# Gated attention in fp32 split products: attention's order from another table, outer sums around the gate's step, first attention loads a step later

## The chip, the cores and the metric

One core of one Trainium2 chip runs the kernel. TensorE (PE) multiplies matrices into PSUM, VectorE (DVE), ScalarE (ACT) and GpSimd (POOL) do elementwise work, SyncE (SP) issues most DMA transfers. The metric is the device time of one execution in microseconds; the text gives the median of the runs.

## The reference

x is 2048 x 640, there are 32 heads of 128, and attention reads the last 512 of 2048 cached positions (W = max(256, 2048 // 4)). Everything is float32.

```python
xn = layernorm(x)                                   # no weights, eps 1e-5
q  = (xn @ wq) as 32 heads of 128
p  = softmax(q @ k[:, -512:].T * 128**-0.5)         # no mask
s  = (p @ v[:, -512:]) as 2048 x 4096 @ wo
h  = relu(xn @ w1 + b1) ** 2                        # 640 -> 1728
g  = silu(h @ w2 + b2)                              # 1728 -> 640
out = x + s * g
```

## The kernel before, in words

Each float32 operand is split into a rounded part (hi, tile index 0) and the remainder (lo, index 1), and each product is three matmuls, hi·hi + hi·lo + lo·hi (`triple`). The hi parts are made by ScalarE copies, the lo parts by a subtraction on VectorE or POOL. All matmuls are 128x128 by 128x512, and 512 rows of x are one tile, so there are four.

The program has three stages. **First**, layer norm and the feed-forward part: the up products of tile 0, then those of tiles 1 and 2 in a seven-product scheme, and the down products of tiles 1 and 2. The down products are the loop over m from 0 to 27 (14 chunks of w2 for tile 1, then 14 for tile 2; `c_down`), called steps below. A step is 15 matmuls into five PSUM banks py. Its operands ch (a block of h) and cw (a block of w2) are loaded three steps ahead on SyncE (`c_load`) and split two steps ahead on ScalarE and VectorE (`c_prep`). Behind step 13 stands `gate`: for each of five banks a sigmoid on ScalarE and a multiply on VectorE into sg. Step 14 writes the same banks, so it waits for sg.

Beside these steps the loop makes the outer tiles: sums of x's tiles 0 and 3 that attention's scheme for q needs (`outer_sum`, six subtractions or additions per part q on VectorE; `outer_hi`, a copy on ScalarE; `outer_lo`, a subtraction on VectorE and two stores to memory). There are two parts, each with its own load (`outer_load`, four DMAs of 0.26 MB). The dictionary OUTER says which of them runs at which step. After the last, their memory becomes the pool "ep", into which attention's first operands are loaded (x as ax, wq as qr, k as kr; `load_raw`, `load_xT`), before attention's first product q_mm(0), which stands ahead of step 27.

**Second**, attention: 128 units (two halves of the rows x 16 groups of two heads x two row tiles x two heads), each 12 matmuls of scores s into two banks, softmax (maxima by VectorE, gathered by ScalarE, exp on ScalarE, the split of p into pt by ScalarE and POOL) and 12 matmuls o. Every second unit adds five products r with wo, added to acc. q comes from the same seven-product scheme, group by group: products into banks pq..a and pq..b, between them a copy qp of b, a copy of a into b (`q_seed`), and sums `q_add`, `q_sum` (qu) on VectorE. In the first half POOL and ScalarE also prepare the sums of wq (gr, zs) for the second half.

**Third**, the feed-forward part of tile 3, and the output.

The order in attention is set by a plan: each operation gets a time, `at(when, f, *a)`, in periods of 12.4 per unit, plus offsets from the table K; operations are recorded sorted by that time, and each engine keeps its recorded order (class Ordered). The times are no measured times: they only set the order. For q_seed:

```python
on(key("Q4", 8.3), q_seed, n)
```

where `key` adds the offsets K["Q4" + ...] for the third of the run, the place in the group and the unit. Every operation is issued through Ordered, so line 322 of the profile is nearly all of them; the groups are told apart by their tiles.

Of the kernel before, what the change touches and what calls it, by code (L numbers as in the profile page):

```python
# [11 lines left out]
ALU = mybir.AluOpType  # L12
# [12 lines left out]
K = {  # L25
# [68 lines left out]
    "ZK3": 0.45, "ZKa": -0.8, "ZKb": 1.81, "ZKc": 7.72, "ZKd": 3.31, "ZKe": 4.57, "ZL0": -0.89,  # L94
    "ZL1": -1.83, "ZL2": -1.23, "ZL3": 0.77, "ZLa": 0.33, "ZLb": 2.02, "ZLc": 6.28, "ZLd": 0.51,
# [173 lines left out]
def kernel(  # L269
# [20 lines left out]
    DC = D // P  # L290
# [876 lines left out]
    for q in range(NQ2):  # L1167
# [4 lines left out]
        if q == 0:  # L1172
            steps += [(len, ())] * int(K.get("OG", 0))
# [1153 lines left out]
```

## Time and profile before

| | us |
|---|---|
| median of 3 runs | 1945.45 |
| lowest, highest | 1944.21, 1947.82 |
| profiled execution, its own time | 1943.89 |
| its span | 1942.1 |
| TensorE busy | 1921.4 |
| VectorE busy | 1673.9 |
| POOL busy | 1490.1 |
| ScalarE busy | 1423.8 |

Busy times are of the whole span. The profile's rows name an operation as out<-in with the buffers' numbers left out, so pq, o, r and s are the products described above and py those of the down steps. "x12" is a count. In the timeline a row gives the start, the duration, the engine, and in brackets how long the engine sat idle before and for whom.

### The profile page before, as it was taken

The numbers are of one execution on the slowest core, as the hardware profiler recorded it, in microseconds if no ns is written. First come the engines' busy times: TensorE is split into PE (matmuls) and PEld (weight loads), VectorE is DVE, ScalarE is ACT, GpSimd is POOL, SyncE is SP. The second block draws the span as 40 slices with busy tenths as digits, with TensorE's granted clock in tenths as the row PEclk, the third lists the DMA queues.
The fourth block names the chain that finished last, engine by engine and source line by source line (L and its number), as shares of the span: only waits on it lengthen the run. The fifth ranks groups of instructions, "written<-read, shape, count | busy, mean of one in ns | idle before, by whom it ended". The sixth has DMA issues, their size and how long they took to land. (4 is left out here: it accounts for less than half of the span.)

```text
span 1942.1 us, 30037 instructions
## 1 busy us (share of the span) xinstructions
PE 1921.4 (99%) x8405; PEld 1563.8 (81%) x8405; DVE 1673.9 (86%) x2451; ACT 1423.8 (73%) x3096; POOL 1490.1 (77%) x963
## 2 busy tenths in 40 slices
PE   9999999999999999999999999999999999999998
PEld 7888778778888888888887788888888888888887
DVE  6864756899999999999999889999999999999865
ACT  5665536888888888888887788777777777777743
POOL 1022116999999999999998888999998888888952
PEclk9999999999999999999999999999999999999999
DMA  6866885654444444444457632333332222222455
GB/s 204 275 216 215 302 320 185 201 161 146 148 147 147 147 147 147 147 147 147 147 159 236 197 112 75 106 106 106 106 116 85 85 85 85 85 85 87 140 167 199
DMA packets 195409, 296.97 MB, mean 153 GB/s; under 512 B 19044, under 2 KB 100726, under 8 KB 194230
## 3 DMA queue, kind: packets, MB, share of 16 engines
q1 hardware_dynamic: 190102, 275.77, 44.2%
q0 software_dynamic: 5008, 19.14, 2.5%
q8 instruction: 77, 1.26, 0.3%
q14 instruction: 78, 0.64, 0.1%
q10 hardware_dynamic: 144, 0.16, 0.0%
HBM read 219.49 MB, written 75.51 MB: 152 GB/s over the span
## 5 line engine op out<-in xcount | busy, mean ns | idle before, releaser
L322 POOL TENSOR_TENSOR pt<-e,pt 128x1024 fp32r<-128x1024 f32 x256 | 616.8, 2409 | 87.5 <-ACT pt L322 85.2
L322 PE MATMUL r<-ots,wo 128*128 128x512 f32 x1920 | 489.5, 391 | 1.2 <-ACT acc L322 0.8
L322 PEld LDWEIGHTS r<-ots,wo 128*128 128x128 f32 x1920 | 357.9, 188 | 82.6 <-DVE acc L322 5.4
L322 PE MATMUL o<-pt,wv 128*128 128x512 f32 x1536 | 380.2, 391 | 0.5 <-POOL pt L322 0.4
L322 PE MATMUL s<-q,wk 128*128 128x512 f32 x1536 | 374.4, 391 | 0.2 <-DVE q L322 0.2
L322 PEld LDWEIGHTS o<-pt,wv 128*128 128x128 f32 x1536 | 285.5, 188 | 67.4 <-POOL pt L322 8.7
L322 DVE TRANSPOSE_TENSOR_REDUCE rdm<-s 128x32 f32<-128x1024 f32 x256 | 311.6, 1236 | 32.5 <-PE s L322 26.1
L322 PEld LDWEIGHTS s<-q,wk 128*128 128x128 f32 x1536 | 285.9, 188 | 65.8 <-DVE q L322 5.0
L322 POOL TENSOR_TENSOR e<-e,e 128x1024 f32<-128x1024 f32 x128 | 308.1, 2407 | 8.5
L322 DVE TENSOR_TENSOR e<-s,bm 128x1024 f32<-128x1024 f32 x256 | 302.5, 1183 | 1.9 <-POOL pt L322 0.6
L322 ACT ACTIVATE e<-e 128x1024 f32<-128x1024 f32 x256 | 270.2, 1056 | 45.0 <-DVE e L322 43.9
L322 ACT ACTIVATE pt<-e 128x1024 fp32r<-128x1024 f32 x256 | 270.7, 1057 | 9.7 <-PE o L322 0.2
L322 DVE TENSOR_TENSOR acc<-r,acc 128x512 f32<-128x512 f32 x300 | 198.8, 663 | 11.7 <-PE r L322 11.3
L322 ACT ACTIVATE rdm<-rdm 32x64 f32<-32x64 f32 x384 | 97.8, 255 | 123.1 <-DVE rdm L322 118.1
L322 DVE TRANSPOSE_TENSOR_REDUCE rds<-e 128x32 f32<-128x1024 f32 (+1 forms) x128 | 124.3, 971 | 28.3 <-POOL e L322 27.7
L322 ACT ACTIVATE rowm<-rowm 32x16 f32<-32x16 f32 x384 | 82.2, 214 | 63.9 <-DVE rowm L322 59.7
L322 ACT ACTIVATE rds<-rds 32x32 f32<-32x32 f32 (+1 forms) x384 | 89.3, 232 | 42.4 <-DVE rds L322 37.7
L322 ACT ACTIVATE rows<-rows 32x16 f32<-32x16 f32 x384 | 82.2, 214 | 34.0 <-DVE rows L322 26.5
L322 PE MATMUL py<-ch,cw 128*128 128x512 f32 x410 | 97.3, 399 | 6.6 <-ACT cw L322 4.5
L322 PEld LDWEIGHTS py<-ch,cw 128*128 128x128 f32 x410 | 78.7, 193 | 24.8 <-ACT cw L322 4.9
L322 POOL TENSOR_TENSOR wo<-or,wo 128x640 fp32r<-128x640 f32 x62 | 97.7, 1575 | 0.9 <-ACT wo L322 0.9
L322 DVE STREAM_TRANSPOSE bm<-rowm 128x512 f32<-128x512 f32 x128 | 87.3, 682 | 12.0 <-ACT rowm L322 10.6
(642 smaller groups left out, 3175.9 us busy)
## 6 DMA issues: line engine op xcount, KB each, us to landing
qp<-wq_d SPq DMA_DIRECT2D x60, 640.0 KB
qp<-wq_d SPq DMA_DIRECT2D x60, 512.0 KB
or<-in_wo_dram SPq DMA_DIRECT2D x62, 320.0 KB
kr<-in_kT_dram SPq DMA_DIRECT2D x62, 256.0 KB
vr<-in_v_dram SPq DMA_DIRECT2D x62, 256.0 KB
wq_d<-ots SPq DMA_DIRECT2D x112, 128.0 KB
gr<-in_wq_dram SPq DMA_DIRECT2D x32, 320.0 KB
wq_d<-gr SPq DMA_DIRECT2D x80, 128.0 KB
```

What stands on the lines that cost most here:

```text
L322: ins = method(*args, **kwargs)
```

## The change

Three things.

The table K has other numbers: offsets for the same operations of attention and of the last stage. Their set of operations is the same, their order is not.

OUTER is written out by step. Part 0 runs at steps 10, 11, 12, 14 and 15, part 1 at 17 to 21; before, they were laid out three at a time from step 10 on, so part 0 also had three operations at step 13, ahead of the gate. The second load comes at step 12 instead of 15.

Attention's first loads come one step later, behind the loads for steps 26 and 27, and each tile of x comes in two parts (columns 0 to 2, then 3 and 4) at steps 23 to 26. Before, x's first tile was loaded whole at step 22 and its second at 24.

```diff
 K = {
-    "Q412": 5.0, "Q42": 2.37, "Q422": 0.73, "Q4@10": 1.41, "Q4@122": 3.21, "Q4@58": 1.52,
+    8.97, "Q42": 0.4, "Q422": 2.63, "Q4@10": 1.79, "Q4@122": 1.93, "Q4@58": 0.11, "Q4@6": -2.14,
...
-    steps = []
-    for q in range(NQ2):
-        steps += [(outer_sum, q, k) for k in range(3)]
-        steps += [(outer_hi, q, 0), (outer_sum, q, 3), (outer_sum, q, 4), (outer_hi, q, 1)]
-        steps += [(outer_lo, q, 0), (outer_sum, q, 5), (outer_hi, q, 3), (outer_lo, q, 1), (outer_hi, q, 2)]
-        steps += [(outer_lo, q, 3), (outer_lo, q, 2)]
-        if q == 0:
-            steps += [(len, ())] * int(K.get("OG", 0))
-    first_m, per = int(K.get("OM", 11)), K.get("OP", 3.0)
-    for n, w in enumerate(steps):
-        OUTER.setdefault(int(first_m + n / per), []).append(w)
+    OUT0, OUT1 = 10, 17
+    for q, first in enumerate((OUT0, OUT1)):
+        for n, *w in (
+            *((0, outer_sum, q, k) for k in range(3)),
+            *((1, outer_hi, q, 0), (1, outer_sum, q, 3), (1, outer_sum, q, 4)),
+            *((2, outer_hi, q, 1), (2, outer_lo, q, 0), (2, outer_sum, q, 5)),
+            *((4 - q, outer_hi, q, 3), (4 - q, outer_lo, q, 1), (4 - q, outer_hi, q, 2)),
+            *((5 - q, outer_lo, q, 3), (5 - q, outer_lo, q, 2)),
+        ):
+            OUTER.setdefault(first + n, []).append(tuple(w))
...
-        if m == first_m + int((len(steps) / per + K.get("OG", 0) / per) / 2) - 1 + int(K.get("OX", 0)):
+        if m == OUT0 + 2:
             outer_load(1)
-        if m == OPEN + int(K.get("OO", 0)):
-            for f, *a in [w for n, l in sorted(OUTER.items()) if n >= m for w in l]:
-                f(*a)
-            OUTER.clear()
+        if m == OPEN + 1:
+            assert not OUTER
             octx.close()
             pools["ep"] = ctx.enter_context(tc.tile_pool(name="early", bufs=1, side="right"))
+        n = m - OPEN - 1
+        if n == 1:
             load_raw("q", 0, 0)
             load_raw("k", 0, 0)
             open_xT(0, 0)
+        for t, c in {0: ((0, slice(0, 3)),), 1: ((0, slice(3, DC)),), 2: ((1, slice(0, 3)),), 3: ((1, slice(3, DC)),)}.get(n - 1, ()):
+            if (t, c.start) == (1, 0):
+                open_xT(0, 1)
             for i in range(2):
-                load_xT(0, 0, i, slice(0, DC))
-        if m == OPEN + 2 + int(K.get("OO", 0)):
+                load_xT(0, t, i, c)
+        if n == 2:
             for kind in "qk":
                 prep(kind, 0, 0, dve)
                 load_raw(kind, 0, 1)
-            open_xT(0, 1)
-            for i in range(2):
-                load_xT(0, 1, i, slice(0, DC))
-        if m == OPEN + 4 + int(K.get("OO", 0)):
+        if n == 4:
```

OPEN is 21; the table before had OM 10, OG 6 and OO 1. The engines and queues that the table could choose for these operations are written in, the same ones.

Three places show what moves. The first is VectorE ahead of the gate, before (to is an outer tile, ch15 and cw15 are the operands of step 15, sg the gate's result):

```order
L322 TENSOR_TENSOR to021_2406<-xc3_2_2268,xc3_0_2148 128x512
L322 TENSOR_TENSOR ch15_1_2507<-ch15_2469,ch15_0_2506 128x512
L322 TENSOR_TENSOR cw15_1_2511<-cw15_2467,cw15_0_2510 128x640
L322 TENSOR_TENSOR to011_2404<-to011_2404,to010_2403 128x512
L322 SCALAR_TENSOR_TENSOR sg_2535<-py1_0_2087,b_sb_65,sg_2535 128x512
L322 SCALAR_TENSOR_TENSOR sg_2539<-py1_1_2088,b_sb_65,sg_2539 128x512
L322 SCALAR_TENSOR_TENSOR sg_2543<-py1_2_2089,b_sb_65,sg_2543 128x512
```

and with the change:

```order
L322 TENSOR_TENSOR to021_2406<-xc3_2_2268,xc3_0_2148 128x512
L322 TENSOR_TENSOR ch15_1_2512<-ch15_2469,ch15_0_2511 128x512
L322 TENSOR_TENSOR cw15_1_2516<-cw15_2467,cw15_0_2515 128x640
L322 SCALAR_TENSOR_TENSOR sg_2535<-py1_0_2087,b_sb_65,sg_2535 128x512
L322 SCALAR_TENSOR_TENSOR sg_2539<-py1_1_2088,b_sb_65,sg_2539 128x512
L322 SCALAR_TENSOR_TENSOR sg_2543<-py1_2_2089,b_sb_65,sg_2543 128x512
L322 SCALAR_TENSOR_TENSOR sg_2547<-py1_3_2090,b_sb_65,sg_2547 128x512
L322 SCALAR_TENSOR_TENSOR sg_2551<-py1_4_2091,b_sb_65,sg_2551 128x512
L322 TENSOR_TENSOR ch16_1_2561<-ch16_2509,ch16_0_2560 128x512
L322 TENSOR_TENSOR cw16_1_2565<-cw16_2507,cw16_0_2564 128x640
L322 TENSOR_TENSOR to011_2404<-to011_2404,to010_2403 128x512
```

The subtraction for to011 stood ahead of sg and now stands behind the operands of step 16.

The second is SyncE around attention's first loads, before:

```order
L322 DMA cw25_2820<-in_w2_dram 128x640
L322 DMA ch25_2822<-h_m2_11_204 128x512
L322 DMA qr0_0_2836<-in_wq_dram 128x640
L322 DMA kr0_0_2838<-in_kT_dram 128x512
L322 DMA ax0_0_0_2840<-xT_d0_0_66 128x2560
L322 DMA ax0_0_1_2841<-xT_d0_1_67 128x2560
L322 DMA cw26_2859<-in_w2_dram 128x640
L322 DMA ch26_2861<-h_m2_12_205 128x512
L322 DMA cw27_2863<-in_w2_dram 128x640
L322 DMA ch27_2865<-h_m2_13_206 128x512
L322 DMA qr0_1_2901<-in_wq_dram 128x640
L322 DMA kr0_1_2907<-in_kT_dram 128x512
```

and with the change:

```order
L322 DMA cw25_2820<-in_w2_dram 128x640
L322 DMA ch25_2822<-h_m2_11_204 128x512
L322 DMA cw26_2851<-in_w2_dram 128x640
L322 DMA ch26_2853<-h_m2_12_205 128x512
L322 DMA cw27_2855<-in_w2_dram 128x640
L322 DMA ch27_2857<-h_m2_13_206 128x512
L322 DMA qr0_0_2867<-in_wq_dram 128x640
L322 DMA kr0_0_2869<-in_kT_dram 128x512
L322 DMA ax0_0_0_2871<-xT_d0_0_66 128x1536
L322 DMA ax0_0_1_2872<-xT_d0_1_67 128x1536
L322 DMA ax0_0_0_2871<-xT_d0_0_66 128x1024
L322 DMA ax0_0_1_2872<-xT_d0_1_67 128x1024
```

The loads for steps 26 and 27 stood behind x's first tile (ax0_0) and now stand ahead of qr, kr and x, and x comes in smaller pieces.

The third is ScalarE in attention, unit 26, before (pq7b<-pq7a is q_seed for group 7, e the exponentials, pt their hi part):

```order
L322 ACTIVATE e26_0_6702<-e26_0_6702 128x1024
L322 ACTIVATE pt26_0_0_6720<-e26_0_6702 128x1024
L322 ACTIVATE e26_1_6718<-e26_1_6718 128x1024
L322 ACTIVATE qp57_6726<-pq7b_6651 128x512
L322 ACTIVATE pt26_1_0_6729<-e26_1_6718 128x1024
L322 ACTIVATE pq7b_6732<-pq7a_6668 128x512
L322 ACTIVATE ots0_3064<-zs8_2_6700 128x2x128
```

and with the change:

```order
L322 ACTIVATE e26_0_6712<-e26_0_6712 128x1024
L322 ACTIVATE pt26_0_0_6722<-e26_0_6712 128x1024
L322 ACTIVATE qp57_6728<-pq7b_6657 128x512
L322 ACTIVATE e26_1_6730<-e26_1_6730 128x1024
L322 ACTIVATE pq7b_6742<-pq7a_6666 128x512
L322 ACTIVATE pt26_1_0_6750<-e26_1_6730 128x1024
L322 ACTIVATE ots0_3068<-zs8_2_6704 128x2x128
```

The copy qp57 moved ahead of e26_1, and pq7b ahead of pt26_1_0. Two moves go the other way: on TensorE the three matmuls pq9a<-ax0_0 of group 9 (and their like in 12 groups of the first half) moved from behind the six of r33_0 to directly behind s36_2, and on VectorE qu324 (and its like in 13 groups of the second half) moved from ahead of the lo part of ots2 to behind it.

More of the change, by code (lines that the diff above doesn't have):

```diff
@@ L25 @@
 K = {
[68 rows of a table removed]
-    "ZK3": 0.45, "ZKa": -0.8, "ZKb": 1.81, "ZKc": 7.72, "ZKd": 3.31, "ZKe": 4.57, "ZL0": -0.89,
-    "ZL1": -1.83, "ZL2": -1.23, "ZL3": 0.77, "ZLa": 0.33, "ZLb": 2.02, "ZLc": 6.28, "ZLd": 0.51,
[169 rows of a table removed]
[67 rows of a table added]
+    1.27, "ZHc": 5.54, "ZHd": -16.51, "ZHe": 4.38, "ZK1": 1.35, "ZK2": -2.2, "ZK3": 0.71, "ZKa":
+    -0.77, "ZKb": 2.09, "ZKc": 8.07, "ZKd": 3.54, "ZKe": 5.95, "ZL0": -1.19, "ZL1": 0.06, "ZL2":
+    -1.49, "ZL3": 1.69, "ZLa": -0.05, "ZLb": 0.49, "ZLc": 4.46, "ZLd": 2.86, "ZLe": 4.2, "ZR0":
[169 rows of a table added]
 }
@@ L1126, in outer_load @@
             for i in range(2):
-                (pool, sp)[int(K.get("OLX", 0))].dma_start(XO[q][:, j, i, :], xT_d[0][i][:, NQ2 * j + q, :])
+                sp.dma_start(XO[q][:, j, i, :], xT_d[0][i][:, NQ2 * j + q, :])
     def outer_tiles(q):
@@ L1150, in outer_sum @@
         )[k]
-        ENG["o"].tensor_tensor(out, one, two, op=op)
+        dve.tensor_tensor(out, one, two, op=op)
     def outer_hi(q, j):
@@ L1158, in outer_lo @@
         hi, lo = TO[q][j]
-        ENG["l"].tensor_tensor(lo, raw(lo), raw(hi), op=ALU.subtract)
+        dve.tensor_tensor(lo, raw(lo), raw(hi), op=ALU.subtract)
         for i in range(2):
-            (pool, sp)[int(K.get("OLS", 0))].dma_start(TS_d[0][j][:, q, i, :], raw(TO[q][j][i]))
+            pool.dma_start(TS_d[0][j][:, q, i, :], raw(TO[q][j][i]))
     XO, TO = {}, {}
-    ENG = {"o": (dve, pool)[int(K.get("OE", 0))], "l": (dve, pool)[int(K.get("OL", 0))]}
     OUTER = {}
-    steps = []
-    for q in range(NQ2):
-        steps += [(outer_sum, q, k) for k in range(3)]
-        steps += [(outer_hi, q, 0), (outer_sum, q, 3), (outer_sum, q, 4), (outer_hi, q, 1)]
-        steps += [(outer_lo, q, 0), (outer_sum, q, 5), (outer_hi, q, 3), (outer_lo, q, 1), (outer_hi, q, 2)]
-        steps += [(outer_lo, q, 3), (outer_lo, q, 2)]
-        if q == 0:
-            steps += [(len, ())] * int(K.get("OG", 0))
-    first_m, per = int(K.get("OM", 11)), K.get("OP", 3.0)
-    for n, w in enumerate(steps):
-        OUTER.setdefault(int(first_m + n / per), []).append(w)
+    OUT0, OUT1 = 10, 17
[8 more added lines that the diff above has]
+            OUTER.setdefault(first + n, []).append(tuple(w))
     XT, ACC, KT, VV, WQ, WO, Q, E, SC, MB, RD, PT, PO, OT, RB, QPS, FX, CL, PRS, RAW = (
@@ L1881 @@
             pools["to"] = octx.enter_context(tc.tile_pool(name="outer", bufs=1, side="right"))
-        if m == first_m - 2 + int(K.get("OX0", 0)):
+        if m == OUT0 - 2:
             outer_load(0)
-        if m == first_m + int((len(steps) / per + K.get("OG", 0) / per) / 2) - 1 + int(K.get("OX", 0)):
+        if m == OUT0 + 2:
             outer_load(1)
-        if m == OPEN + int(K.get("OO", 0)):
-            for f, *a in [w for n, l in sorted(OUTER.items()) if n >= m for w in l]:
-                f(*a)
-            OUTER.clear()
+        if m == OPEN + 1:
+            assert not OUTER
             octx.close()
             pools["ep"] = ctx.enter_context(tc.tile_pool(name="early", bufs=1, side="right"))
+        n = m - OPEN - 1
+        if n == 1:
             load_raw("q", 0, 0)
```

471 rows, old and new, of the table K are left out of this document.

## The prediction

> **What bounds the kernel now.** I read the page first, then the waits of TensorE, then its windows, and only where these showed lost time the timeline.
>
> ```profile
> span 1942.1 us, 30037 instructions
> ...
> PE 1921.4 (99%) x8405; PEld 1563.8 (81%) x8405; DVE 1673.9 (86%) x2451; ACT 1423.8 (73%) x3096; POOL 1490.1 (77%) x963
> ```
>
> TensorE is the bound: 99% busy with 8405 matmuls, whose number the change leaves alone. So the change can win only time in which TensorE waits or runs at half clock, and can lose only by new waits. Where it waits (us in total, times, longest):
>
> ```profile
> PE py L322 <- ACT cw L322: 4.5, 1, 4.5
> PE py L322 <- DVE sg L322: 1.9, 1, 1.9
> ...
> PE pq16a L322 <- DVE qu L322: 1.0, 1, 1.0
> PE r L322 <- ACT acc L322: 0.8, 2, 0.6
> ...
> PE pq2a L322 <- ACT pq2b L322: 0.4, 1, 0.4
> ```
>
> This list understates. A matmul is drawn 0.39 us long, but back to back they start 0.227 apart (below: 42 in 9.68 us, so 9.29 / 41), so each wait costs 0.16 more than it shows, and one below 0.16 shows nothing. I therefore count matmuls by window, attention alone (330 to 1905 us; a row gives the stretch, its length, busy us and count of TensorE, its weight loads, VectorE, ScalarE and POOL, then granted clock, DMA share and GB/s):
>
> ```profile
> 330.00:395.00 65.00, 63.71 (x276) 51.13 (x275) 53.81 (x74) 55.83 (x130) 60.61 (x41) 1.00 0.62 194
> 395.00:990.00 595.00, 593.92 (x2583) 478.06 (x2582) 561.81 (x786) 479.08 (x1111) 557.17 (x383) 1.00 0.47 146
> 990.00:1160.00 170.00, 167.93 (x730) 135.10 (x729) 153.87 (x218) 133.47 (x305) 149.35 (x96) 1.00 0.58 183
> 1160.00:1535.00 375.00, 375.00 (x1646) 307.62 (x1645) 342.28 (x498) 290.59 (x637) 340.34 (x183) 1.00 0.31 99
> 1535.00:1635.00 100.00, 100.00 (x442) 82.54 (x441) 92.56 (x135) 76.50 (x169) 88.37 (x47) 1.00 0.27 91
> 1635.00:1905.00 270.00, 269.76 (x1187) 221.77 (x1186) 232.29 (x330) 186.50 (x401) 218.18 (x120) 1.00 0.36 117
> ```
>
> A window also counts matmuls that hang over its edge, 1.7 of them (0.39 / 0.227). The fifth window is the pace: 100 / (442 - 1.7) = 0.2271 us. By that pace the others should take 62.3, 586.2, 165.4, 373.4 and 269.2 us; they take 2.7, 8.8, 4.6, 1.6 and 0.8 more: **18.5 us** that attention loses in small pieces.
>
> **The change part by part.** *First loads a step on, x in four parts.* The longest wait stands ahead of step 26 of the down loop:
>
> ```profile
> 261.77 19.20 PE L322 MATMUL py<-ch,cw 128*128 128x512 f32 x84
> ...
> 271.00 0.33 SPq L322 DMA_DIRECT2D qr<-in_wq_dram  x1
> ...
> 271.86 0.90 SPq L322 DMA_DIRECT2D ax<-xT_d  x2
> ...
> 273.28 0.43 SPq L322 DMA_DIRECT2D ch<-h_m  x1
> ...
> 284.13 0.63 ACT L322 ACTIVATE ch<-ch 128x512 fp32r<-128x512 f32 x1 [12.81 <-DMA ch<-h_m]
> ...
> 285.44 5.19 PE L322 MATMUL py<-ch,cw 128*128 128x512 f32 x15 [4.47 <-ACT cw L322]
> ...
> 293.88 3.56 PE L322 MATMUL py<-ch,cw 128*128 128x512 f32 x15
> ```
>
> The load of ch for step 26 is issued behind two loads of x of 1.31 MB each (128x2560 in four bytes), and ScalarE waits 12.81 us for it. In the change SyncE issues the loads for steps 26 and 27 ahead of qr, kr and all of x. The wait goes: 4.47 + 0.16, and with it the slow run behind it, 5.19 - 3.56 = 1.63. **6.2 us**; between 3.6 (x still slows what is left, and the half clock stays) and 6.3.
>
> What is late next is x itself, for attention's first product, which stands behind step 26.
>
> ```profile
> 237.40:240.84 3.44, 1.56 (x7) 1.16 (x7) 3.44 (x6) 3.44 (x7) 2.76 (x6) 1.00 0.97 257
> 240.84:244.25 3.41, 3.41 (x9) 2.68 (x9) 3.41 (x6) 1.07 (x2) 1.18 (x3) 0.50 1.03 396
> ...
> 1080.50:1083.90 3.40, 2.37 (x11) 1.67 (x10) 3.40 (x6) 1.67 (x6) 3.40 (x2) 1.00 0.92 313
> 1083.90:1087.30 3.40, 3.40 (x16) 2.79 (x16) 3.17 (x7) 1.86 (x8) 3.32 (x5) 1.00 0.24 78
> ...
> 273.00:285.00 12.00, 7.97 (x36) 6.26 (x34) 0.21 (x1) 0.87 (x2) 0.00 (x0) 1.00 0.96 368
> ```
>
> The last of these rows: DMA moves 368 GB/s when it is full. qr, kr (0.33 and 0.26 MB) and the first tile of x, 2.62 MB, are 3.2 MB, so 8.7 us. SyncE is held until 271.00, when the outer tiles' memory is free; that stays about so (one pair more of their stores moves to the last step, about 1 us). So x is in at about 281. Step 26 without its wait ends at 280.97 + 15 x 0.227 = 284.4, or 282 with the gate's gain below. A margin of 1 to 3 us, and each us that x is late costs one: between 0 and 2, I take 0. The second tile of x follows by 290, before the third unit needs it.
>
> *The gate's step without outer sums.* Step 14 waits for the first sg:
>
> ```profile
> 227.82 9.68 PE L322 MATMUL py<-ch,cw 128*128 128x512 f32 x42
> ...
> 237.24 0.82 DVE L322 TENSOR_TENSOR cw<-cw,cw 128x640 fp32r<-128x640 f32 x1
> ...
> 237.98 0.69 DVE L322 TENSOR_TENSOR to<-to,to 128x512 fp32r<-128x512 f32 x1
> ...
> 238.58 3.38 DVE L322 SCALAR_TENSOR_TENSOR sg<-py,b_sb,sg 128x512 f32<-128x512 f32 x5
> ...
> 239.38 6.92 PE L322 MATMUL py<-ch,cw 128*128 128x512 f32 x22 [1.88 <-DVE sg L322]
> ```
>
> VectorE runs without a gap here, and only the "to" operation leaves its row ahead of sg: sg starts at 237.98, 0.6 sooner. ScalarE loses two operations there too and has its half of sg ready. So the wait shrinks from 1.88 to about 1.3. The 22 matmuls behind it took 6.92 where pace gives 21 x 0.227 + 0.39 = 5.16: 1.76 lost to the half clock in the second window row above. Does the half clock stay? After an idle of 1.88 in a 3.4 us window it came, after 1.03 (the row at 1080.50) it did not. 1.3 is nearer to 1.03, so I count it as gone: 0.6 + 1.8 = **2.4 us**, between 0.6 and 3.8.
>
> The Trainium skill (TensorE: Matmul & The Clock Gate, "What's actually happening") has the clock drop after at least one idle window of about 3.4 us. By that rule neither 1.88 nor 1.3 would halve it; the trace disagrees with the first (0.50 after 1.88). By the rule the term would be 0.6 with nothing to win back, by the row 2.4; the row decides.
>
> The second outer load also moves, from step 15 to 12: 1.05 MB ahead of the loads for step 16, under 3 us at 368 GB/s, with ScalarE at those tiles only behind the gate. I cost it at nothing; without that cover it would be a wait of at most 3 us.
>
> *Attention's places.* No operation is added or removed; the table moves about 590 matmuls and some 900 operations of the other engines past neighbours. What returns most often, here in group 7:
>
> ```profile
> 628.24 2.88 PE L322 MATMUL s<-q,wk 128*128 128x512 f32 x12
> ...
> 629.60 1.05 ACT L322 ACTIVATE pt<-e 128x1024 fp32r<-128x1024 f32 x1
> ...
> 630.55 0.59 ACT L322 ACTIVATE pq7b<-pq7a 128x512 f32<-128x512 f32 x1
> ...
> 631.20 0.98 PE L322 MATMUL pq7b<-ax,qp 128*128 128x512 f32 x3
> ```
>
> After the s block the next matmul was due at 628.24 + 12 x 0.227 = 630.96; it started at 631.20, when ScalarE's copy was done, and the third ran 0.13 late once more: 0.37 per group. The change puts the copy ahead of pt, 1.05 us earlier. Groups 4 to 14 have this, so 11 x 0.37 = 4.0. The long waits go alike: the copy for pq2a moves ahead of two operations of 1.05, six matmuls (1.36) now stand between s and the r that waited 0.6, and the sum qu for pq16a moves ahead of an operation of 0.65 against a wait of 1.03 that I count as half gone; 2.0 in the first window, 2.9 of 4.6 in the third. Of what is left of the second window (4.8) I take a third, 1.6; of the 2.4 behind 1160, where POOL's pt moves ahead of a weight's operation, half, 1.2. Together 2.0 + 4.0 + 1.6 + 2.9 + 1.2 = 11.7.
>
> Against it stand two new neighbourhoods:
>
> ```profile
> 739.80 1.53 PE L322 MATMUL s<-q,wk 128*128 128x512 f32 x6
> ...
> 740.52 0.64 DVE L322 TENSOR_TENSOR qu<-pq9a,qp 128x512 f32<-128x512 f32 x1
> ...
> 741.16 1.52 PE L322 MATMUL r<-ots,wo 128*128 128x512 f32 x6
> ...
> 1466.82 0.69 DVE L322 TENSOR_TENSOR qu<-pq24a,qp 128x512 f32<-128x512 f32 x1
> ...
> 1467.98 0.84 PE L322 MATMUL pq24a<-ax,qp 128*128 128x512 f32 x3
> ```
>
> In 12 groups of the first half the pq products that overwrite what qu reads now come directly behind s, at 741.16, the moment qu ends: the six r matmuls that gave 1.36 of room stand behind them. In 13 groups of the second half qu comes behind one more operation (ots, 0.67) with 0.47 of room. Per group 0 to 0.4 us, so 0 to 10 in all. In both places the sums ahead of qu also move earlier (rowm ahead of a 1.25 reduction; r, on which VectorE's acc waits, by three matmuls), so I take the low side, 2.2. Attention: 11.7 - 2.2 = **9.5 us**, between 0 and 16.
>
> The sum: 6.2 + 2.4 + 9.5 = 18.1. The profiled execution took 1943.89 (span 1942.1 and 1.8 around it), so 1925.8. It was 1.56 below the median of the runs shown, 1945.45; against that median **1927**.
>
> **Rivals.**
> *Attention gives it back.* VectorE is busy 561.8 of 595 us in the second window. If its chain, not TensorE, sets the pace of the first half, the room won at the copies returns as a wait for qu. For it: the 10 us bound above. Against: 33 us of idle. Only loads, gate and 0 to 4 of attention remain: 1933 to 1939, about 1936.
> *All of it clears.* Gate 3.8, attention 14 to 16: about 1920. Against: the two new neighbourhoods.
> *No change.* Both tiles of x and the raw weights are 6.4 MB, 17 us of DMA at 368 GB/s from 271 on. If other loads share that, TensorE reaches attention 8.6 us sooner and waits there, and attention's moves cancel: 1942 to 1949. Against: the first product needs only the first half of these bytes.
> *Slower.* The wait for qu in the first half's 12 groups is a large one. If VectorE comes to qu one reduction and one sum later (1.25 + 0.68), TensorE stands 1.9 + 0.2 in each: 25 us, with 4.8 from the second half 30, against 20.3 won without the new waits: 1955. It decides from 1.3 us per group; beyond 1.6 the kernel is slower by 0.2%. For it: VectorE is the fullest engine behind TensorE. Against: nothing that long moves ahead of qu there.
>
> **How the numbers follow.** Forecast (1922 to 1932) 0.56; attention gives back 0.22; all clears 0.07; no change 0.09; slower 0.06. A measurement here cannot tell less than 0.2% (3.9 us) from no change. Faster by more: 0.56 + 0.22 + 0.07 = 0.85; same 0.09; slower 0.06. The range runs from 1920, the attention bound of 16 with the early terms, to 1940, the early terms without the clock and without attention (6.8); it leaves out the last two cases and half of the best one, 0.18.
>
> **What would show it.** Right: no wait of TensorE on ACT cw in the step before attention, and full clock from 285 on; at the gate a wait near 1.3 with full clock behind; attention's window of 595 us doing its 2581 matmuls in some 589; pq4b to pq14b without a wait. Wrong: TensorE waiting on DVE qu in many groups; a wait of the first pq on a load of ax; a new wait at step 16; half clock still there behind the gate.

## The result and the profile after

The changed kernel takes 1926.66 us (median of 4 runs, 1924.03 to 1927.98) against 1944.83 before (4 runs, 1942.46 to 1947.82): a ratio of 0.9904, 95% interval 0.9887 to 0.9922. That is 18.7 us less (15 to 22), where the sum of the prediction had 18.1. The time is as forecast; its parts are not, as the rest of this text shows.

The page of the changed kernel first, then the longest of TensorE's waits in it (us in total, times, longest):

```profile
span 1922.3 us, 30072 instructions
...
PE 1907.6 (99%) x8405; PEld 1568.5 (82%) x8405; DVE 1668.1 (87%) x2451; ACT 1437.0 (75%) x3096; POOL 1491.0 (78%) x963
```

```profile
PE pq L322 <- DMA ax<-xT_d: 3.0, 3, 2.1
```

The span fell by 19.8 us and TensorE's busy time by 13.8 of these, with the same 8405 matmuls: most of the gain was late starts too short to show as idle time, and half clock, which no list of waits shows. The wait for cw (4.5) is gone. A wait for ax, attention's tiles of x, stands in its place.

Attention by windows, about the stretches of the prediction, 10 to 20 us earlier (length, busy us and count of TensorE, weight loads, VectorE, ScalarE, POOL, granted clock, DMA share, GB/s):

```profile
320.00:378.00 58.00, 57.98 (x255) 47.54 (x255) 49.24 (x67) 50.65 (x119) 56.69 (x37) 1.00 0.62 191
378.00:970.00 592.00, 592.00 (x2610) 489.07 (x2609) 564.05 (x790) 492.03 (x1118) 562.63 (x384) 1.00 0.48 151
970.00:1142.00 172.00, 171.23 (x751) 139.82 (x749) 158.38 (x227) 137.55 (x317) 153.87 (x100) 1.00 0.57 185
1142.00:1520.00 378.00, 378.00 (x1664) 311.41 (x1663) 345.61 (x503) 296.64 (x644) 345.19 (x186) 1.00 0.31 101
1520.00:1620.00 100.00, 100.00 (x442) 82.42 (x441) 92.14 (x137) 77.43 (x171) 87.80 (x47) 1.00 0.24 82
1620.00:1887.00 267.00, 266.80 (x1175) 219.52 (x1174) 227.15 (x325) 186.96 (x396) 216.29 (x118) 1.00 0.37 121
```

With the pace of 0.2271 us and 1.7 matmuls taken off each count, these matmuls should take 57.5, 592.3, 170.2, 377.5, 100.0 and 266.5 us: attention now loses 3 us in all (0.5, 0, 1.8, 0.5, 0, 0.5), where it lost 18.5. Of the two new neighbourhoods nothing is left to see but 0.1 us at a time. By the starts of the matmuls in both traces (what is more than 0.02 us beyond the pace), the late ones of the kernel before were o with 4.1 us in all, pq4b to pq14b behind the copies with 3.9, r with 3.7 and s with 2.5; with the change they are o with 0.9 and r with 1.4, and the other two are all but gone.

The gate in the timeline (start, duration, engine, and in brackets the idle time before and its releaser):

```profile
236.84 0.82 DVE L322 TENSOR_TENSOR cw<-cw,cw 128x640 fp32r<-128x640 f32 x1
237.58 3.38 DVE L322 SCALAR_TENSOR_TENSOR sg<-py,b_sb,sg 128x512 f32<-128x512 f32 x5
...
238.37 7.79 PE L322 MATMUL py<-ch,cw 128*128 128x512 f32 x33 [1.34 <-DVE sg L322]
```

sg follows cw directly and the wait is 1.34. The 33 matmuls behind it take 7.79 us where full clock gives 32 x 0.227 + 0.39 = 7.65, so the clock was not halved. And the entry to attention (the two loads of cw belong to steps 26 and 27, ts_d are the stores of the outer tiles):

```profile
247.81 14.54 PE L322 MATMUL py<-ch,cw 128*128 128x512 f32 x57
...
264.74 0.33 SPq L322 DMA_DIRECT2D cw<-in_w_dram  x1
...
266.68 0.33 SPq L322 DMA_DIRECT2D cw<-in_w_dram  x1
...
267.55 1.60 POOL L322 DMA_DIRECT2D ts_d<-to  x3 [0.87 <-DVE to L322]
...
276.67 0.33 SPq L322 DMA_DIRECT2D qr<-in_wq_dram  x1
...
285.30 0.47 PE L322 MATMUL pq<-ax,wq 128*128 128x512 f32 x1 [2.09 <-DMA ax<-xT_d]
286.43 2.31 PE L322 MATMUL pq<-ax,wq 128*128 128x512 f32 x9 [0.65 <-DMA ax<-xT_d]
288.95 1.45 PE L322 MATMUL pq<-ax,wq 128*128 128x512 f32 x5 [0.22 <-DMA ax<-xT_d]
290.24 3.58 PE L322 MATMUL py<-ch,cw 128*128 128x512 f32 x15
```

The first row holds small waits at the starts of steps 18 and 20: 57 matmuls at pace take 56 x 0.227 + 0.39 = 13.1, so 1.4 is lost. SyncE was to be free at 271 to 272; it issues qr at 276.67. Step 26 ends at 283.2, and the 15 products behind it take until 290.24 instead of 3.4 us: 3.6 lost. Two windows tell what SyncE waited for:

```profile
266.00:274.00 8.00, 8.00 (x37) 6.60 (x37) 5.72 (x9) 3.37 (x5) 2.28 (x5) 1.00 0.95 328
274.00:277.50 3.50, 3.50 (x17) 2.92 (x16) 0.42 (x1) 0.00 (x0) 0.00 (x0) 1.00 0.07 30
```

The DMA is nearly full until 274. In these 8 us the queue of SyncE's loads moves 1.17 MB, what the loads for steps 26 and 27 amount to, and the queue of POOL's stores 1.43 MB, the outer tiles; the two share the DMA. Then it falls nearly idle until qr and x are let through. What lets them through is the landing of the last store. Of the eight stores of the second part, here with the times from issue to landing, it is the slowest:

```profile
DMA to landing us min/median/max: 3.8/5.6/7.9
```

It lands at 276.52, 7.9 us after its issue (3.5 in the kernel before), and qr goes out 0.14 us behind that, here and in each of the fourteen profiled executions of this text.

### The profile page after: what moved, and what is told of

It reads as the page before. It is cut to its first block, busy times and chain, and to the rows that moved or that the text cites. A ratio compares the mean times of both kernels' runs of the same rounds, so it can differ in the third digit from the quotient of the medians.

```text
span 1922.3 us, 30072 instructions
## 1 busy us (share of the span) xinstructions
PE 1907.6 (99%) x8405; PEld 1568.5 (82%) x8405; DVE 1668.1 (87%) x2451; ACT 1437.0 (75%) x3096; POOL 1491.0 (78%) x963
## 5 line engine op out<-in xcount | busy, mean ns | idle before, releaser
L322 ACT ACTIVATE pt<-e 128x1024 fp32r<-128x1024 f32 x256 | 271.0, 1059 | 13.1 <-PE o L322 0.4
L322 DVE STREAM_TRANSPOSE bs<-rows 128x512 f32<-128x512 f32 x128 | 89.2, 697 | 24.2 <-ACT rows L322 24.2
```

What stands on the lines that cost most here:

```text
L322: ins = method(*args, **kwargs)
```

## Experiments

Each ratio is to the kernel before, with its 95% interval; microseconds are the ratio's distance from 1 times 1944.8.

### The three parts alone

The table alone (the kernel before with K replaced, OG and OLX kept):

```diff
 K = {
...
+    "OG": 6, "OLX": 1,
```

> The kernel before with the new numbers for attention and nothing else of the change. By the trace of the changed kernel, in which nearly every wait of TensorE in attention is gone, the numbers alone are worth 14 to 15 us: about 1930.3, and TensorE still waits 4.5 for cw in step 26 and 1.9 at the gate. By the sum of the prediction (9.5 us) it would be 1935.3. If instead part of attention's gain came from loads that land sooner, the waits on pq2b, pq4b to pq14b would be back.

1929.16 us, ratio 0.9923 (0.9910 to 0.9936): 15.0 us, 12.4 to 17.5. Attention's gain comes from its order alone, and it is half as large again as the 9.5 of the sum. The wait for cw stays (line 323 of this kernel is line 322 of the others):

```profile
PE py L323 <- ACT cw L323: 4.4, 1, 4.4
```

The loads alone (the kernel before with the load block of the change):

```diff
+        n = m - OPEN - 1
+        if n == 1:
             load_raw("q", 0, 0)
...
             for i in range(2):
-                load_xT(0, 0, i, slice(0, DC))
-        if m == OPEN + 2 + int(K.get("OO", 0)):
+                load_xT(0, t, i, c)
+        if n == 2:
...
```

> The kernel before with the change to attention's first loads alone (a step on, behind the loads for steps 26 and 27, x in four parts); outer tiles and attention's numbers as before. Theory of the prediction: SyncE is free at 271, x is in by 281, the wait of 4.5 for cw and the half clock behind it go, and the time is 1938.6. Theory from the changed kernel's trace: the loads of steps 26 and 27 stand ahead of the last stores on the DMA, SyncE is held until about 275, x is in at about 284 against 284.4 for the end of step 26: a gain of 5 to 6, 1939 to 1940, with a wait below 1 on ax. If the half clock does not hang on the wait, only 4.6 are won, 1940.2, and the granted clock is below 1 near 285.

1938.06 us, ratio 0.9976 (0.9962 to 0.9989): 4.7 us, 2.1 to 7.4. From the timeline of the profiled execution, the fastest of seven (1936.05 to 1944.09):

```profile
264.90 0.54 POOL L322 DMA_DIRECT2D ts_d<-to  x1 [0.41 <-DVE to L322]
...
272.38 0.33 SPq L322 DMA_DIRECT2D qr<-in_wq_dram  x1
...
281.53 3.70 PE L322 MATMUL pq<-ax,wq 128*128 128x512 f32 x15
285.06 3.58 PE L322 MATMUL py<-ch,cw 128*128 128x512 f32 x15
```

The wait for cw and the half clock behind it are gone, and the list of waits has none for ax. In this execution the prediction's first term holds, with x just in time: qr goes out at 272.38. What the slower executions met is not known.

The outer tiles alone (the kernel before with OUTER written out as changed and the second load at step 12):

```diff
-        if m == first_m + int((len(steps) / per + K.get("OG", 0) / per) / 2) - 1 + int(K.get("OX", 0)):
+        if m == OUT0 + 2:
             outer_load(1)
```

> The kernel before with the new places of the outer tiles alone (parts at steps 10, 11, 12, 14, 15 and 17 to 21, second load at step 12); loads of attention and numbers as before. By the prediction: the gate's wait falls by 0.6 and the half clock goes, 2.4 us less, 1942.4. By the traces since: the gate's wait was 1.3 to 1.9 in three executions of the old places and halved the clock in one of them, so 0.3 to 1 is won there; SyncE is freed one step's stores later, about 272, and the wait for cw in step 26 grows by about 1: 1944 to 1946, no difference.

1948.23 us, ratio 1.0016 (1.0007 to 1.0025): **3.1 us slower** (1.4 to 4.9), where no difference was expected. The profiled execution is the slowest of eleven (1952.45), so its waits are larger than the mean cost:

```profile
250.90 0.47 PE L322 MATMUL py<-ch,cw 128*128 128x512 f32 x1 [0.62 <-DVE ch L322]
...
275.14 0.33 SPq L322 DMA_DIRECT2D qr<-in_wq_dram  x1
...
290.48 6.10 PE L322 MATMUL py<-ch,cw 128*128 128x512 f32 x15 [8.07 <-ACT cw L322]
```

With the second part at steps 17 to 21, TensorE waits for operands behind the gate (0.62 for ch), the last stores go out 3.7 us later, SyncE is freed at 275.14, and the wait for cw is 8.07 instead of 4.47. The three parts add up: 15.0 + 4.7 - 3.1 = 16.6 against 18.7 for all of them, within the intervals.

### What holds SyncE

The second outer part a step earlier:

```diff
-    OUT0, OUT1 = 10, 17
+    OUT0, OUT1 = 10, 16
```

> The changed kernel with the second part of the outer tiles at steps 16 to 20 instead of 17 to 21. Theory: SyncE is held until 276.7 because the last stores of the outer tiles are issued at 268.6, behind the loads for steps 26 and 27, which fill the DMA until 274.5. Then stores a step earlier go ahead of these loads, SyncE issues qr by about 271, x is in before step 26 ends, and the 3.6 us ahead of the first products go: about 1923. Rival: what holds SyncE is not those stores, or the loads share the DMA with them all the same: qr still at 275 to 277 and the time stays 1926.7. A cost that could hide it: VectorE has three sums more at step 16, behind the gate, and TensorE waits up to 2 us for cw or ch there.

1920.62 us (1919.68 to 1922.35), ratio 0.9883 (0.9870 to 0.9897): by the ratios some 4 us less than the changed kernel. The two intervals overlap a little; the single times don't, but they are of different series, in which the median of the kernel before lay between 1943.3 and 1945.6.

```profile
251.74 31.51 PE L322 MATMUL py<-ch,cw 128*128 128x512 f32 x135 [0.25 <-ACT cw L322]
283.08 3.56 PE L322 MATMUL pq<-ax,wq 128*128 128x512 f32 x15
286.49 3.56 PE L322 MATMUL py<-ch,cw 128*128 128x512 f32 x15
...
273.64 0.33 SPq L322 DMA_DIRECT2D qr<-in_wq_dram  x1
```

None of attention's first products waits any more: 3.41 us for the 15. The wait at the gate is 0.33 in this execution, another 1.0 us less than in the changed kernel's. SyncE is free 3 us sooner, not 5.7: the last stores are issued 2.8 earlier (from 264.78 on), but the two steps' loads still share the DMA with them, and the last one takes 7.7 us to land. Small waits behind the gate remain (2.0 us between 241 and 264).

The load for step 27 behind the first part of x:

```diff
-        for n in {OPEN + 2: (m + 3, m + 4), OPEN + 3: ()}.get(m, (m + 3,)):
+        for n in (m + 3,):
```

> The changed kernel with the loads for step 27 issued one step later, behind the first part of x's first tile, so that only the loads for step 26 stand ahead of the outer tiles' last stores. Theory: 0.59 MB less on the DMA ahead of those stores is 1.6 us at 368 GB/s, so SyncE issues qr at about 275 instead of 276.7, and TensorE's waits for ax ahead of attention's first products shrink from 3.0 to 1 or 2; step 27 finds its operands: 1925. Rival: the stores' landing does not depend on these loads; qr stays at 276.7 and the time at 1926.7, or step 27 now waits for cw and it is 1928.

1924.07 us, ratio 0.9889 (0.9875 to 0.9903). The wait for ax is 1.2 instead of 3.0, and the time lies 2.9 below the changed kernel's, which the intervals can't tell apart. SyncE's qr goes out at 275.99, although this execution issues its last stores 2 us later than the changed kernel's. Over all fourteen executions, from the end of the last issue of ts_d to qr: with neither step's loads ahead of the stores 2.8 to 4.3 us (six executions, the kernel before among them: 267.94 to 271.00), with step 26's alone 4.8 (one), with both 6.5 to 7.8 (seven, the changed kernel among them: 269.15 to 276.67). So **the loads that were put ahead of x delay the stores that x waits for**, by 3.5 us in the mean; by an estimate from the prediction's row, their 1.18 MB take 3.2 us at 368 GB/s.

x in whole tiles:

```diff
-        for t, c in {0: ((0, slice(0, 3)),), 1: ((0, slice(3, DC)),), 2: ((1, slice(0, 3)),), 3: ((1, slice(3, DC)),)}.get(n - 1, ()):
+        for t, c in {0: ((0, slice(0, DC)),), 2: ((1, slice(0, DC)),)}.get(n - 1, ()):
```

> The changed kernel with each tile of x loaded whole instead of in two parts, at the step of its first part. Theory: SyncE is free at 276.7 as before, and the first product now waits for the whole tile, which is in at about 288.8 instead of 285.3 for the first three columns: 1.5 to 2.3 us more, 1928.5. Rival: the parts do not matter, since the last columns land at the same time either way and the products catch up: 1926.7.

1928.06 us, ratio 0.9909 (0.9895 to 0.9924): the timed difference from the changed kernel (1.4) is less than can be told. In the trace:

```profile
286.70 0.49 PE L322 MATMUL pq<-ax,wq 128*128 128x512 f32 x1 [2.28 <-DMA ax<-xT_d]
289.08 5.69 PE L322 MATMUL pq<-ax,wq 128*128 128x512 f32 x14 [1.89 <-DMA ax<-xT_d]
```

The products wait for the hi tile and then for the lo tile, 4.2 instead of 3.0, and 14 of them take 5.69 for 13 x 0.227 + 0.39 = 3.34, at half clock. So where x is late, its parts are worth about 1 us by these two executions, and 2 more in one in which the clock falls.

### The outer tiles' places

All of them back to where they were, in the changed kernel:

```diff
-        if m == OUT0 + 2:
+        if m == 15:
             outer_load(1)
```

(and OUTER laid out three at a time, as before.)

> The changed kernel with the outer tiles' steps and the second load as they were before; loads of attention and numbers as changed. Theory: the new places of the outer tiles are the harmful part of the change. With the old ones the last stores go 2 to 3 us earlier, SyncE issues qr by about 272.5, no product waits for ax, and the small waits at steps 18 and 20 (1.4 us) are not there: ahead of attention TensorE loses 1 to 2 us instead of 4 to 5, the gate's wait of 1.3 to 2.5 among them, 1921 to 1922. By the prediction (gate 2.4 us, x costs nothing): 1929. If the two cancel: 1926.7.

1921.87 us, ratio 0.9886 (0.9873 to 0.9900), as the theory had it: by the ratios 3.5 less than the changed kernel, with intervals that overlap. One step of the theory failed: qr went out at 274.24, not 272.5, and 1.5 us of waits for ax are left.

The first part as changed, the second and its load as before, except that the last subtraction and its stores stand at step 20 instead of 21:

```diff
-    for q, first in enumerate((OUT0, OUT1)):
+    for q, first in ((0, OUT0),):
...
+    for n, *w in (
+        *((16, outer_sum, 1, 0), (17, outer_sum, 1, 1), (17, outer_sum, 1, 2), (17, outer_hi, 1, 0)),
...
```

> The changed kernel with the first outer part as changed (nothing at the gate's step) and the second part and its load as they were before. Theory: the gate's wait falls to 0.3 to 1.3 and the rest is as in the run with all outer tiles put back: 1920 to 1921, the fastest of all. Rival: with the first part's last five operations behind the gate, the second part starts late and its stores with it, SyncE is held past 275 and ax is waited for: 1923 to 1925.

1921.15 us, ratio 0.9885 (0.9872 to 0.9899). Here the wait at the gate is 0.23, and with its stores a step earlier than in the run with all outer tiles put back, qr goes out at 271.76 instead of 274.24. This one, the step-16 version and the one with all outer tiles put back can't be told apart (0.9883 to 0.9886); none of their single times, which are of other series, is as long as the changed kernel's lowest, 1924.03.

### The gate

In the changed kernel, the first part's three operations of step 14 back at step 13, ahead of the gate:

```diff
-            *((4 - q, outer_hi, q, 3), (4 - q, outer_lo, q, 1), (4 - q, outer_hi, q, 2)),
+            *((3, outer_hi, q, 3), (3, outer_lo, q, 1), (3, outer_hi, q, 2)),
```

> The changed kernel with three operations of the first outer part put back from step 14 to step 13, ahead of the gate. Theory of the prediction: the wait for sg is 1.9 again instead of 1.3 and with it comes half clock for one window of 3.4 us: 2.4 us more than the changed kernel, 1929.1. Rival: the half clock was no matter of the wait's length: the wait grows by 0.6 and the clock stays at 1.00, 1927.3. A second rival: the operand of the last outer sum was the only thing in sg's way, the wait does not grow, 1926.7.

1923.94 us, ratio 0.9898 (0.9881 to 0.9914): no slower than the changed kernel. The extra operation stands ahead of sg as it should, and yet:

```profile
238.84 7.36 PE L322 MATMUL py<-ch,cw 128*128 128x512 f32 x31 [1.49 <-DVE sg L322]
```

1.49 and full clock. Over the other thirteen executions the gate's wait scatters by more than the 0.6 that the edit moves: with the old places 1.21 to 2.53 (seven, mean 1.67), with the new ones 0.23 to 1.82 (six, mean 1.15). Half clock followed the gate in two of the fourteen, one with either places.

### Attention: single waits

The copy ahead of pt, and nothing else, in the kernel before (a shift of the second pt in one unit of each group):

```diff
-    "h122": 0.08
+    "h122": 2.82
```

(and h1@58, h1@62, h1@66 lowered by the same 2.74, to keep the places of those units.)

> The kernel before with one number moved, so that on ScalarE the second pt of a unit stands behind q_seed's copy in groups 2 to 14 of the first half and nothing else changes its place. By the prediction: 0.37 us in each of 11 groups (4 to 14) and 0.5 at pq2b, 4.5 us in all, 1940.3, with no wait left on pq4b to pq14b. Rival: pt comes 0.6 us later, POOL's lo part of it with it, and TensorE waits as long for pt at o: 1944.8. Second rival: the time won in a group is lost at the next wait of the same group (r for acc, pq for qu): 1943 to 1944.

1946.54 us, ratio 1.0007 (0.9998 to 1.0016): nothing won. Then the wk swap on top (wk is prepared later, so that on POOL the lo part of pt goes ahead of wk's):

```diff
+    "Pk01": 1.17
```

> The kernel before with two swaps in the groups of the first half: on ScalarE the second pt stands behind q_seed's copy (which alone won nothing), and the operation that prepares wk stands later, so that on POOL the second pt's lo part goes ahead of wk's (1.29 us). Theory: POOL ran without idle time up to that lo part, and the wait for it at o took back what the copy gave; with both swaps 0.4 to 0.5 us in each of 11 groups go, 4 to 5 us: 1940. Rival: the wait moves on once more, to wk at the next scores or to qu, and the time stays within 1 us of 1945.

1948.64 us, ratio 1.0028 (1.0015 to 1.0040): 5.4 us slower (2.9 to 7.8). In the profiled execution 0.3 is won in the ten groups shown below, and 2.3 are lost ahead of them and 2.2 behind them; the cause of these stays open. And VectorE's rowm ahead of rds, alone in the kernel before:

```diff
-    "rm23": -0.31
+    "rm23": -0.65
```

> The kernel before with one swap: in one unit of each group of the first half, VectorE's and ScalarE's rowm stands ahead of rds (a reduction of 1.25 us) instead of behind it; the copies and pt stay where they were. Theory: groups of the first half took 48.40 us in the kernel before and in both runs that moved the copy and pt, whatever TensorE then waited for, and 47.63 in the changed kernel; what sets 48.40 is VectorE's chain, which loses 0.73 at bm for the late rowm. So this swap alone brings groups to 47.7 and wins 8 to 9 us, and the waits for the copy shrink without being touched: 1935.5. By the prediction, in which each wait stands for itself, the copies' waits of 0.37 stay and the swap wins nothing or at most 4: 1940 to 1944. Between them (47.63 + 0.37 = 48.0 a group): 1939.5.

1944.48 us, ratio 0.9995 (0.9986 to 1.0004): no difference; the theory that this one swap is the key fell.

Ten groups of the first half (from s of unit 12 to s of unit 52) tell it best; in order, the kernel before, the copy's swap, copy and wk, rowm, the table alone and the changed kernel, each from its own windows:

```profile
446.70:930.74 484.04, 483.21 (x2102) 388.89 (x2100) 457.21 (x641) 388.84 (x900) 453.18 (x310) 1.00 0.48 147
```

```profile
446.96:930.99 484.03, 482.56 (x2102) 389.49 (x2100) 457.25 (x642) 389.90 (x901) 453.20 (x310) 1.00 0.47 147
```

```profile
448.96:932.73 483.77, 483.71 (x2101) 389.96 (x2100) 456.84 (x641) 390.58 (x900) 452.88 (x310) 1.00 0.47 147
```

```profile
446.59:930.06 483.47, 482.54 (x2101) 389.56 (x2100) 458.93 (x642) 389.02 (x900) 454.32 (x311) 1.00 0.48 148
```

```profile
442.10:918.48 476.38, 476.38 (x2102) 393.70 (x2101) 455.92 (x641) 395.02 (x901) 453.87 (x311) 1.00 0.48 150
```

```profile
439.99:916.37 476.38, 476.38 (x2102) 393.79 (x2101) 455.90 (x641) 394.85 (x901) 453.87 (x311) 1.00 0.48 150
```

The table takes 7.7 us off ten groups; no smaller edit takes off more than 0.6. Yet each did what its edit says, and the lateness moved. By the starts of the matmuls (more than 0.02 us beyond the pace), the groups lose 5.7 us in the kernel before, 3.5 of it at pq..b behind the copies (what is left of the 7.7 comes in smaller pieces). With the copy's swap they lose 6.1, nothing at pq..b and 4.2 at o; with wk on top 5.7, of which r has 3.1 and pq..a 1.7; with rowm's swap 5.7, 3.6 of it at pq..b as before; with the table 0.1. In group 7, with the copy's swap, o waits where pq7b did, and VectorE waits for rowm at bm:

```profile
637.84 1.42 PE L322 MATMUL o<-pt,wv 128*128 128x512 f32 x5 [0.18 <-POOL pt L322]
...
635.76 0.71 DVE L322 STREAM_TRANSPOSE bm<-rowm 128x512 f32<-128x512 f32 x1 [0.73 <-ACT rowm L322]
```

With wk's swap added the nine matmuls of o run through, and r (1.66 for six that take 1.52) and pq7a (the same) are late:

```profile
638.61 2.20 PE L322 MATMUL o<-pt,wv 128*128 128x512 f32 x9
640.78 1.66 PE L322 MATMUL r<-ots,wo 128*128 128x512 f32 x6
...
643.72 1.66 PE L322 MATMUL pq7a<-ta,qp 128*128 128x512 f32 x6
```

With rowm's swap VectorE no longer waits 0.73 for bm, and waits for TensorE instead, which still waits for the copy:

```profile
629.71 1.07 PE L322 MATMUL s<-q,wk 128*128 128x512 f32 x4
630.86 2.37 PE L322 MATMUL pq7b<-ax,qp 128*128 128x512 f32 x9
...
644.20 1.25 DVE L322 TRANSPOSE_TENSOR_REDUCE rdm<-s 128x32 f32<-128x1024 f32 x1 [0.67 <-PE s L322]
```

(Of the four s matmuls the last starts at 630.39, so pq7b was due at 630.62 and came 0.24 late.) The likely reading is that at least two chains held a group at 48.4 us: one through TensorE with the copy or pt in it, one through VectorE with rowm. That would explain why each swap alone wins nothing. It is argued from these rows, not shown: no run has the copy's and rowm's swaps together, and which of the table's moves are needed stays open.

## Why the prediction came out right, and where it did not

*The bound.* TensorE, 99% busy: right, and so was counting by pace and not by listed waits. The 18.5 us that windows gave for attention are what the table could win, and it won all but 3 of them.

*First loads a step on, 6.2 us.* The wait for cw and the half clock went as described, and in the kernel with this part alone they count 4.7. In the changed kernel 3.6 came back as the wait for ax, so the term was worth 2.6. The step that failed is "SyncE is held until 271.00 ... that stays about so": it was held until 276.67, 5.7 longer: the last stores are issued 1.2 later, and from there to qr it takes 4.5 longer, because the moved loads share the DMA with them. The prediction asked what a late x would cost and set its bound at 2; it did not ask what the moved loads do to the stores. A wait of the first pq on ax was one of its own signs of being wrong, and it came.

*The gate, 2.4 us.* The pair of profiled executions agrees with it (1.34, full clock), and that was luck: the wait scatters by more than the change moves it, and half clock behind the gate came in one execution with the old places and in one with the new. The means of the two sets differ by 0.5 us, which is within their scatter.

*The second outer load and the later second part, nothing.* This is the part that costs: 3.1 us alone, and 3.5 by the ratios when undone in the changed kernel. By the traces 1.4 of it are the small waits at steps 18 and 20, and the rest the later stores; this split is argued, not shown, since the step-16 version keeps such waits and is as fast as the versions without them. The prediction priced the load's bytes and the gate; it counted one pair of stores a step later as "about 1 us" and did not look at what the second part meets behind the gate.

*Attention, 9.5 us.* It won 15.0. Both halves were off: the gross gain (11.7) counted fractions of the smaller waits, where nearly all of them went, and the new neighbourhoods (2.2) cost some 0.1 us at a time. The step that failed is the method: "0.37 per group ... 11 x 0.37 = 4.0" takes each wait as an amount of its own. The runs show that the copy's swap is worth nothing by itself, since o is then late instead of pq..b, and that the whole table is worth more than the parts that were counted.

*The rivals.* That attention gives its gain back was not what the change did. It is what the single swaps did, at o and r and not at qu. The case of no change named a wait for x on entering attention as its cause: that wait came, at 3.6 instead of 8.6. Waits for qu, the slower case, did not appear.

That the sum was right is luck: errors cancelled, 3.6 too much at the loads and 1.4 missed behind the gate, against 5.5 too little in attention (2.6 + 2.4 - 1.4 from the two profiled executions and 15.0 from the ratio make 18.6).

## What to carry to other kernels

Before a load is moved ahead of another, see what the other is waiting for: if that is a store, the moved load takes the DMA from it, and the second load comes later than the move alone would make it. In a steady loop, price a reordering by what the period could fall to, not by adding up waits: here a wait that was removed alone turned up at the next engine, and only the period told. And a change of three parts deserves three runs: here two of them won and the third took back 3 us, which the total hid.

## What the hardware showed that was not expected

By these traces the granted clock is decided over windows of 3.41 us on a grid, whose position differs from execution to execution, and the idle time inside one such window counts, not the length of the wait. (In the kernel before, the clock changed at 240.84, 244.25, 285.21 and 288.62: 3.41, 12 x 3.413 and 3.41 apart.) Three windows of the grid in the run with the copy's swap, whose gate wait was 2.53, the longest of all; then two of the run with step 27's load moved, with a wait of 1.82; then two of the changed kernel, around the wait for ax:

```profile
235.70:239.11 3.41, 1.80 (x8) 1.14 (x7) 3.41 (x6) 2.45 (x6) 2.04 (x4) 1.00 0.85 227
239.11:242.52 3.41, 2.49 (x11) 2.02 (x12) 3.41 (x6) 3.41 (x7) 2.24 (x5) 1.00 0.97 328
242.52:245.93 3.41, 3.41 (x17) 2.77 (x16) 3.35 (x7) 1.32 (x3) 1.35 (x3) 1.00 1.04 414
```

```profile
237.19:240.60 3.41, 1.59 (x8) 0.96 (x7) 3.41 (x6) 1.93 (x4) 2.15 (x4) 1.00 0.82 228
240.60:244.01 3.41, 3.41 (x10) 2.65 (x9) 1.72 (x3) 0.00 (x0) 2.17 (x4) 0.50 0.97 361
```

```profile
281.68:285.09 3.41, 1.53 (x7) 0.94 (x5) 1.52 (x3) 0.39 (x1) 0.00 (x0) 1.00 0.95 341
285.09:288.50 3.41, 2.55 (x10) 1.80 (x10) 0.00 (x0) 0.00 (x0) 0.00 (x0) 1.00 1.03 412
```

2.53 us of idle split over two windows (1.61 and 0.92) left the clock at 1.00; 1.82 in one window halved it for the next. In all fourteen executions, up to the program's end, a window at full clock with up to 1.70 idle was never followed by half clock, one with 2.1 and more always was, and between 1.8 and 1.9 both happened: the last two rows have a window with 1.88 idle and one at full clock behind it, while the kernel before had 1.88 at the gate and half clock behind it. Two windows can take up to 1.70 each, so whether a wait of 1.8 to 3.4 us costs half clock hangs on where the grid falls, and one execution can't price it. The Trainium skill (TensorE: Matmul & The Clock Gate, "What's actually happening") has the clock drop after at least one idle window of about 3.4 us; the length of the window agrees with these rows (3.41), but a window little more than half idle was enough.
